# Random-feature attention and two feed-forward layers on one core: query tiles in slots among the keys and in half steps of the first group

## The chip, the core and the metric

The kernel runs on one core of a Trainium2 chip. The metric is the device time of one execution in microseconds. The engines are named as in the profile: PE is TensorE (PEld its weight loads), DVE is VectorE, ACT is ScalarE, POOL is GpSimd, and SP issues the DMAs.

## What is computed

The input has 4 batches of 576 rows, 8 heads of 64 columns. Cut to what matters:

```python
def phi(x):                                   # 128 random features of each head
    h = einsum('bhsd,md->bhsm', x, omega) - sum(x * x, -1, keepdims=True) / 2
    return exp(h - max(h, -1, keepdims=True)) / sqrt(m)
q_p, k_p = phi(q * scale), phi(k * scale)
kv = einsum('bhsm,bhsd->bhmd', k_p, v)        # needs every key of the batch
z = sum(k_p, axis=2)
x = einsum('bhsm,bhmd->bhsd', q_p, kv) / (einsum('bhsm,bhm->bhs', q_p, z)[..., None] + 1e-6)
# first layer, 512 -> 1536 -> 512, after a root-mean-square norm
g = xn @ w_gate
y = (g * sigmoid(g) * (xn @ w_val)) @ w_out
# second layer, 512 -> 2048 -> 512
h = y @ w_in
out = (h * cos(h)) @ w_out2
```

## The kernel before

The 2304 rows are 18 tiles of 128. A tile of keys ("k") is projected onto omega (`project`, L214: 16 matmuls into two PSUM banks), DVE takes the negated maximum of each head (L230), ACT the exponentials (L232), and `kv_product` (L388) adds the product with v into two banks of its batch. A tile of queries ("q") is projected the same way, its features are transposed (`transposed`, L239), copied out of PSUM (`keep_transposed`, L247 and L249), multiplied with kv (`sums`, L259), divided (`quotients`, L269 to L271), squared and normed (`square`, `root`, `norm`), transposed again (`turn`, L297) and put as two parts into a block `xhl` (`put`). Three tiles are a block of 384 rows; there are six blocks, and three buffers for them.

The weights come as float32 in integer form and are turned into a two-part form, chunk by chunk (68 chunks of 512 KB): one DMA, four DVE operations (L153 to L160), two of ACT (L138, L170), two of POOL. `Weights.tick` moves this work on by one of its seven turns a chunk; `pace` calls it at a rate. A finished chunk lies in a ring of RING buffers.

The feed-forward layers multiply two-part numbers with three matmuls a product (`mm3`, L446 to L448). The first layer goes over its 12 columns of 128 in three groups of four; in a group, for each of six blocks, each column is one step: 24 matmuls for gate and value (`gate_val`), then 12 for the output of the step before (`out1`), which accumulate in four banks. So a group has 24 steps. The second layer is 96 steps of 12 and 9 matmuls, in groups of 6, 5 and 5 columns.

The attention before runs in two parts. In the first, a loop over 27 tiles (18 of keys, 9 of queries, a k and a q in turn once the first nine keys are through) has its own PSUM pool (`banks_of(w=4, kv=2, q=2)`) and its own SBUF pool; each kv is also stored in DRAM (`kv_dram`, L435). Work of a tile is put off by whole passes of the loop with `after`. The loop ends only when its last query has gone through all its stages, and three blocks are then complete. Then the PSUM pool is closed and opened anew with `w=4, acc=4`; a second SBUF pool for queries is opened, kv and the norm's gain are loaded a second time (L473, L291), and nine queries run in steps 0 to 14 of the first group by the table `plan`, up to three stages of different tiles per step, after the two products of the step.

Every engine takes its instructions in the order in which the program writes them. SP issues all DMAs from one queue.

Of the kernel before, what the change touches and what calls it, by code (L numbers as in the profile page):

```python
# [33 lines left out]
F32 = mybir.dt.float32  # L34
# [4 lines left out]
AF = mybir.ActivationFunctionType  # L39
# [14 lines left out]
def attention_then_ffn(ctx: ExitStack, tc: tile.TileContext, qT, kT, v, omT, wc1, rms_g, wc2, out, B, H, S, D):  # L54
# [34 lines left out]
    banks = ExitStack()  # L89
    psum = [None, None]  # L90

    def banks_of(**tags):

        banks.close()
        psum[:] = banks.enter_context(tc.tile_pool(name="psum", bufs=1, space=PSUM, reuse_waits="tile")), tags

    def bank(tag, name):
        return psum[0].tile([P, 512], F32, tag=tag, name=name, bufs=psum[1][tag])
# [10 lines left out]
    kv_dram = [dram.tile([P, KVW], F32, name=f"kv_dram{b}") for b in range(B)]  # L109
# [89 lines left out]
    class Attention:  # L199
# [3 lines left out]

        def __init__(self, tile_of, tags, kv):
            self.tile_of, self.tags, self.kv, self.pool = tile_of, tags, kv, None
            self.raw, self.e, self.eT, self.x, self.ps, self.ms = {}, {}, {}, {}, {}, {}
            self.gain = None
# [6 lines left out]
        def project(self, nm, t):  # L214

            x = self.raw.pop((nm, t))
            ps = [bank(self.tags[0], f"{nm}p_ps{t}_{r}") for r in range(2)]
# [17 lines left out]
        def transposed(self, t, r):  # L235
            e = self.e.pop(("q", t, r))
            ps = bank(self.tags[1], f"eT_ps{t}_{r}")
# [4 lines left out]
        def keep_transposed(self, t, r):  # L242
# [3 lines left out]
            if self.pool is not None or r:  # L246
# [5 lines left out]
        def sums(self, t, r):  # L252

            eT = self.eT.pop((t, r))
            ps = bank(self.tags[1], f"num_ps{t}_{r}")
# [19 lines left out]
        def square(self, t):  # L275
            sq = self.tile_of("feat", [P, DM], F32, f"sq{t}")
# [12 lines left out]
        def load_gain(self):  # L289
            self.gain = self.tile_of("gain", [P, DM], F32, f"gain_{self.tags[1]}")  # L290
            nc.sync.dma_start(self.gain, rms_g.rearrange("(o c) -> o c", o=1).to_broadcast([P, DM]))  # L291

        def turn(self, t):
            a = self.x.pop(t)
            ps = self.ps["x", t] = bank(self.tags[0], f"xT_ps{t}")
# [27 lines left out]
    with tc.manual_schedule():  # L323

        banks_of(w=4, kv=2, q=2)
        with tc.tile_pool(name="att", bufs=2, side="right", reuse_waits="tile") as ap:
            depth = {"gain": 1, "raw": 4, "feat": 7, "featT": 4, "mx": 6, "den": 4}
            kv = [ap.tile([P, KVW], F32, name=f"kv{b}", bufs=1) for b in range(B)]
            NV = 3
            vt = [ap.tile([P, H + 1, D], F32, name=f"v{i}", bufs=1) for i in range(NV)]  # L330
            att = Attention(
                lambda what, shape, dt, name: ap.tile(shape, dt, tag=what, name=name, bufs=depth.get(what, 2)),
                ("w", "q"), kv)

            def load_v(t):
                if t < NTILE:
                    nc.sync.dma_start(vt[t % NV][:, 0:H], v[t])
# [7 lines left out]
            nc.sync.dma_start(om, omT)  # L345
            att.load(*tiles[0])
            att.load(*tiles[1])
            load_v(0)
            wts.tick(1)
            att.load(*tiles[2])  # L350
            load_v(1)
            load_v(2)
            att.load_gain()
            for a in vt:
                nc.vector.memset(a[:, H], 1.0)
            for a in kv:
                nc.vector.memset(a[:, H * (D + 1):], 0.0)
            make_identity(nc, ident)
            nc.gpsimd.memset(quarter, 0.25)
            nc.gpsimd.memset(half_pi, math.pi / 2)  # L360
            nc.gpsimd.memset(minus_half, -0.5)
            nc.vector.tensor_scalar(om, om, SCALE, None, op0=ALU.mult)

            acc, waiting, now = {}, {}, [0]

            def after(n, f, *args):

                waiting.setdefault(now[0] + n, []).append((f, args))

            def kv_products(t):  # L370

                e = [att.e.pop(("k", t, r)) for r in range(2)]
                for i, part in enumerate(parts(t)):
                    if i:
                        after(1, kv_product, t, e, *part)
                    else:
                        kv_product(t, e, *part)
                after(len(parts(t)), load_v, t + NV)

            def kv_product(t, e, b, p0, n):  # L380
                end = p0 + n + t * P == (b + 1) * S
                for r in range(2):
                    begin = (b, r) not in acc
                    if begin:
                        acc[b, r] = bank("kv", f"kv_ps{b}_{r}")
                    for h in range(HP):
                        hh = 2 * h + r
                        nc.tensor.matmul(  # L388
                            acc[b, r][:, h * P:(h + 1) * P], e[r][p0:p0 + n, h, :],
                            vt[t % NV][p0:p0 + n, hh::H - hh, :],  # L390
                            start=begin and h == 0, stop=end, skip_group_check=True)
                    if end:
                        keep_kv(b, r)

            def keep_kv(b, r):
                nc.vector.tensor_copy(
                    kv[b][:, 0:H * (D + 1)].rearrange("p (h two d) -> p two h d", two=2, d=D + 1)[:, r],
                    acc.pop((b, r)).rearrange("p (h c) -> p h c", c=P)[:, :, 0:D + 1])
                if r == 1:
                    after(1, nc.sync.dma_start, kv_dram[b], kv[b])  # L400

            UP = 15
            s = 0
            while s < len(tiles) or waiting:
                now[0] = s
                if s < len(tiles):
                    att.project(*tiles[s])
                    if s + AHEAD < len(tiles):
                        att.load(*tiles[s + AHEAD])
                if 0 <= s - 2 < len(tiles):  # L410
                    nm, t = tiles[s - 2]
                    if nm == "k":
                        kv_products(t)
                    else:
                        for r in range(2):
                            att.transposed(t, r)
                            after(0, att.keep_transposed, t, r)
                        for r in range(2):
                            after(1, att.sums, t, r)
                            after(1, att.quotients, t, r)  # L420
                        after(2, att.square, t)
# [354 lines left out]
```

## Time and profile before

| | |
|---|---|
| median of 3 runs | 1065.45 us (1064.0 to 1065.6) |
| profiled execution | 1066.04 us, span 1064.2 us |
| PE busy in the span | 95% |
| DVE, ACT, POOL busy | 59%, 44%, 18% |
| mean granted clock of TensorE | 0.987 |

Times below are in microseconds from the start of the span. PE's busy time is modelled from pipelined matmuls, so a stretch is judged by how long its known number of matmuls takes, and by what the idle time in it waited for.

### The profile page before, as it was taken

How to read it: one execution, taken by the hardware profiler on the slowest of the kernel's cores; microseconds unless marked ns; L12 is line 12 of the kernel's file. 1: busy time of each engine (PE TensorE's matmuls, PEld its weight loads, DVE VectorE, ACT ScalarE, POOL GpSimd, SP SyncE). 2: the span in 40 equal slices, each digit the busy share in tenths (PEclk: the TensorE clock that was granted, in tenths of full speed). 3: DMA queues.
4: the chain of work that ended last, by engine and by line, in shares of the span. 5: the costliest groups of instructions: out<-in, count | busy, mean ns of one | idle time of the engine just before them, and what ended most of it. 6: DMA issues, size and time to landing. Idle time of an engine off the chain costs nothing.

```text
span 1064.2 us, 15514 instructions
## 1 busy us (share of the span) xinstructions
PE 1015.5 (95%) x6040; PEld 956.5 (90%) x6040; DVE 632.6 (59%) x1185; ACT 464.9 (44%) x1005; POOL 195.2 (18%) x163
## 2 busy tenths in 40 slices
PE   6787869999999999999999999999999999999998
PEld 6776759999899999999999999999999888999997
DVE  6698743545452444432565644878766888656655
ACT  6576626466632222221233323555544444444443
POOL 3343101121111132220223210221101232000000
PEclk9899979999999999999999999999999999999999
DMA  7555241223132344440345342332220441103401
GB/s 259 210 182 168 110 171 60 71 74 115 50 110 109 135 152 149 149 158 1 103 175 222 115 159 89 129 119 99 99 79 22 173 163 61 60 1 110 156 32 59
DMA packets 33624, 123.96 MB, mean 116 GB/s; under 512 B 3728, under 2 KB 10000, under 8 KB 28944
## 3 DMA queue, kind: packets, MB, share of 16 engines
q1 hardware_dynamic: 33552, 122.99, 32.0%
q8 instruction: 47, 0.77, 0.3%
q14 instruction: 25, 0.20, 0.1%
HBM read 93.46 MB, written 29.51 MB: 116 GB/s over the span
## 4 chain that ended last, share of the span: by engine, by line
PE 77%; DVE 13%; ACT 5%; DMA 2%; issue 2%; SPq 0%; POOL 0%; ACTq 0%; DVEq 0%; POOLq 0%
PE gv_ps L447 9%; PE gv_ps L446 9%; PE gv_ps L448 9%; PE h_ps L448 5%; PE h_ps L446 5%; PE h_ps L447 5%; PE o_ps L447 5%; PE o_ps L448 5%; PE o_ps L446 5%; PE y_ps L446 5%; PE y_ps L447 4%; PE y_ps L448 4%; PE kv_ps L388 2%; PE num_ps L259 2%; DVE turns L592 1%
## 5 line engine op out<-in xcount | busy, mean ns | idle before, releaser
L446 PE MATMUL gv_ps<-xhl,w 128*128 128x384 f32 x576 | 194.1, 337 | 1.4 <-DVE xhl L309 1.4
L447 PE MATMUL gv_ps<-xhl,w 128*128 128x384 f32 x576 | 193.8, 336 | 0.0
L448 PE MATMUL gv_ps<-xhl,w 128*128 128x384 f32 x576 | 193.7, 336 | 0.0
L164 POOL TENSOR_TENSOR f<-f,raw 128x512 f32<-128x512 f32 x68 | 92.5, 1360 | 527.2 <-issue 325.7
L554 DVE TENSOR_TENSOR gv<-gv_ps,gv 128x384 f32<-128x384 f32 x72 | 40.1, 557 | 216.6 <-PE gv_ps L448 186.2
L448 PE MATMUL h_ps<-yhl,w 128*128 128x384 f32 x384 | 129.5, 337 | 0.0
L446 PE MATMUL h_ps<-yhl,w 128*128 128x384 f32 x384 | 129.2, 337 | 0.0
L447 PE MATMUL h_ps<-yhl,w 128*128 128x384 f32 x384 | 129.0, 336 | 0.0
L446 PE MATMUL o_ps<-w,o 128*128 128x512 f32 x288 | 112.4, 390 | 2.5 <-DVE osum L531 2.5
L448 PE MATMUL o_ps<-w,o 128*128 128x512 f32 x288 | 114.2, 397 | 0.2
L447 PE MATMUL o_ps<-w,o 128*128 128x512 f32 x288 | 113.7, 395 | 0.0
L172 POOL TENSOR_TENSOR w<-f,w 128x512 fp32r<-128x512 f32 x68 | 92.6, 1363 | 102.9 <-DVE t L557 49.0
L446 PEld LDWEIGHTS gv_ps<-xhl,w 128*128 128x128 f32 x576 | 109.3, 190 | 2.3 <-DVE xhl L309 1.8
L597 ACT ACTIVATE turns<-turns,half_pi 128x384 f32<-128x384 f32 x96 | 59.2, 617 | 115.6 <-DVE turns L592 115.6
L447 PEld LDWEIGHTS gv_ps<-xhl,w 128*128 128x128 f32 x576 | 109.1, 189 | 0.1
L448 PEld LDWEIGHTS gv_ps<-xhl,w 128*128 128x128 f32 x576 | 109.1, 189 | 0.0
L446 PE MATMUL y_ps<-t,w 128*128 128x384 f32 x288 | 98.9, 343 | 0.8 <-DVE y L519 0.8
L555 ACT CAST t<-gv 128x384 fp32r<-128x384 f32 x72 | 37.0, 514 | 143.4 <-DVE gv L554 143.4
L448 PE MATMUL y_ps<-t,w 128*128 128x384 f32 x288 | 96.8, 336 | 0.0
L447 PE MATMUL y_ps<-t,w 128*128 128x384 f32 x288 | 96.8, 336 | 0.0
L552 ACT ACTIVATE gv<-gv_ps 128x384 f32<-128x384 f32 x72 | 35.4, 492 | 140.4 <-PE gv_ps L448 136.5
L602 DVE TENSOR_TENSOR o<-turns,o 128x384 fp32r<-128x384 f32 x96 | 58.0, 604 | 47.6 <-ACT o L600 47.5
(75 smaller groups left out, 1797.1 us busy)
## 6 DMA issues: line engine op xcount, KB each, us to landing
raw<-wc SPq DMA_DIRECT2D x68, 512.0 KB, 3.6
yhl<-y_dram SPq DMA_DIRECT2D x14, 1536.0 KB, 6.9
xhl<-x_dram SPq DMA_DIRECT2D x10, 1536.0 KB, 7.1
x_dram<-xhl SPq DMA_DIRECT2D x6, 1536.0 KB, 6.1
y_dram<-yhl SPq DMA_DIRECT2D x6, 1536.0 KB, 5.4
kraw<-kT SPq DMA_DIRECT2D x18, 256.0 KB, 4.3
v<-v SPq DMA_DIRECT2D x18, 256.0 KB, 4.2
qraw<-qT SPq DMA_DIRECT2D x18, 256.0 KB, 4.1
```

Of the source, the lines that this page charges most:

```text
L164: nc.gpsimd.tensor_tensor(f32(f), f32(f), rest, op=ALU.add)
L172: nc.gpsimd.tensor_tensor(t[:, 1], self.f.pop(c - 1), f32(t[:, 0]), op=ALU.subtract)
L259: nc.tensor.matmul(ps[p0:p0 + n, h * P:(h + 1) * P], eT[:, h, p0:p0 + n], self.kv[b][:, at:at + P], start=True, stop=True, skip_group_chec ...
L388: nc.tensor.matmul(acc[b, r][:, h * P:(h + 1) * P], e[r][p0:p0 + n, h, :], vt[t % NV][p0:p0 + n, hh::H - hh, :], start=begin and h == 0, s ...
L446: nc.tensor.matmul(o, w[0], x[0], start=first, stop=False)
L447: nc.tensor.matmul(o, w[0], x[1], start=False, stop=False)
L448: nc.tensor.matmul(o, w[1], x[0], start=False, stop=last)
L552: nc.scalar.activation(a, ps[0], AF.Silu)
L554: nc.vector.tensor_tensor(a, ps[1], a, op=ALU.mult)
L555: nc.scalar.copy(t[:, 0], a)
L597: nc.scalar.activation(r, r, AF.Sin, bias=half_pi)
L602: nc.vector.tensor_tensor(o[:, 1], r, f32(o[:, 0]), op=ALU.subtract)
```

## The change

The attention's loop is replaced by slots. Slots 0 to 22 stand ahead of the first layer: 18 tiles of keys, and queries 0 to 4 in slots 6, 9, 12, 15 and 22. From there a slot is half a step of the first group (one product with its half of `out1`), and queries 5 to 17 begin in half steps 1, 3, 6, 9, 11, 14 and so on, 8/3 apart. Stage i of a query stands i slots after its projection, `kv_product` one slot after that of its keys. Stages 4 and 6 stand ahead of the slot's projection or product, all others behind it. Loads run two tiles ahead (three before), with three buffers (four before). Weights move on by four turns a slot until nine chunks are done (by five a pass until 15, before).

One PSUM pool of 4, 2 and 2 banks serves the whole kernel; the sums of the layers use the banks of "kv" and "q" in turn. From slot 23 on, all stages of a query use the four banks "w", which the products use too. One SBUF pool of the attention stays until the sums of the second group need its place, so kv and gain are loaded once. The ring has 22 buffers for 24. The second layer's groups have 5, 6 and 5 columns.

```diff
-    RING = 24
+    RING = 22
-    GROUPS2 = [range(0, 6), range(6, 11), range(11, 16)]
-    EARLY = 3 * TPB
+    GROUPS2 = [range(0, 5), range(5, 11), range(11, 16)]
...
+    BANKS = {"w": 4, "kv": 2, "q": 2}
+    psum = ctx.enter_context(tc.tile_pool(name="psum", bufs=1, space=PSUM, reuse_waits="tile"))
+    def bank_of_sums(name):
+        i = sums_taken[0]
+        sums_taken[0] += 1
+        return bank("kv" if i % 4 < 2 else "q", name)
...
-    kv_dram = [dram.tile([P, KVW], F32, name=f"kv_dram{b}") for b in range(B)]
...
-            depth = {"gain": 1, "raw": 4, "feat": 7, "featT": 4, "mx": 6, "den": 4}
+        depth = {"gain": 1, "raw": 3, "feat": 6, "mx": 6, "den": 4}
...
-            tiles = [("k", t) for t in range(TPP)]
-            for j in range(EARLY):
-                tiles += [("k", TPP + j), ("q", j)]
-            AHEAD = 3
+        tiles = {s: ("k", s) for s in range(6)}
+        tiles.update({6: ("q", 0), 9: ("q", 1), 12: ("q", 2), 15: ("q", 3), 22: ("q", 4)})
+        for t in range(6, NTILE):
+            tiles[next(s for s in range(99) if s not in tiles)] = ("k", t)
+        SLOTS = len(tiles)
+        for t in range(5, NTILE):
+            tiles[SLOTS + 1 + (8 * (t - 5)) // 3] = ("q", t)
+        for s, (nm, t) in tiles.items():
+            if nm == "k":
+                for i in range(len(parts(t))):
+                    then.setdefault(s + 1 + i, []).append((1, kv_product, t, i))
+            else:
+                for i in range(1, 7):
+                    then.setdefault(s + i, []).append((-i, query_step, t, i))
+        AHEAD = 2
+        def slot_before(s):
+            at = order.index(s) if s in tiles else -1
+            if at >= 0 and at + AHEAD < len(order):
+                att.load(*tiles[order[at + AHEAD]])
+            for k, f, *args in then.get(s, []):
+                if k in (-6, -4):
+                    f(*args)
+        def slot_after(s):
+            if s in tiles:
+                att.project(*tiles[s])
+                for r in range(2):
+                    att.features(*tiles[s], r)
+            for k, f, *args in then.get(s, []):
+                if k not in (-6, -4):
+                    f(*args)
         att.load(*tiles[0])
         att.load(*tiles[1])
         load_v(0)
         wts.tick(1)
-            att.load(*tiles[2])
         load_v(1)
         load_v(2)
         att.load_gain()
...
+        UP = 9
+        for s in range(SLOTS):
+            slot_before(s)
+            slot_after(s)
+            if wts.done < UP:
+                wts.tick(4)
+        att.tag = "w"
...
-            hid[n] = gate_val(blk, f, rate / 2)
-            for t, s in plan.get(n, []):
-                query_step(t, s)
+            if g == 0 and n < G:
+                rate = max(rate, 8)
+            s = SLOTS + 2 * n
+            slot_before(s)
+            ps = product(blk, f, 0)
+            a = silu(blk, f, ps)
+            slot_after(s)
             if n >= 1:
-                out1(g0, b0, f0, hid.pop(n - 1), st, en)
+                out1(*steps[n - 1][:3], hid[n - 1], *steps[n - 1][3:], (0, 1))
+            wts.pace(rate / 2)
+            flush(3)
+            slot_before(s + 1)
+            ps = product(blk, f, 1)
+            hid[n] = gated(blk, f, a, ps)
+            slot_after(s + 1)
+            if n >= 1:
+                out1(*steps[n - 1][:3], hid.pop(n - 1), *steps[n - 1][3:], (2, 3))
```

Three places in the instruction order show the move. In the names, `kp`/`qp` are projections, `kmx`/`qmx` maxima, `eT` transposed features, `num` the sums, `xT` the turned tile, `gv` and `y` the products and sums of the first layer; the first number is the tile or block.

SP, between the attention's first part and the first layer, before:

```order
L317 DMA x_dram0_1431<-xhl0_1052 128x3072
L435 DMA kv_dram3_77<-kv3_89 128x584
L317 DMA x_dram1_1629<-xhl1_1433 128x3072
L317 DMA x_dram2_1655<-xhl2_1631 128x3072
L291 DMA gain_w_1668<-rms_g 128x512
L473 DMA kv_in2_1670<-kv_dram2_76 128x584
L211 DMA qraw9_1672<-qT 128x512
L211 DMA qraw10_1731<-qT 128x512
L132 DMA raw19_1769<-wc1 128x1024
```

and of the change, around slots 20 to 23:

```order
L338 DMA v2_91<-v 128x512
L210 DMA qraw4_1121<-qT 128x512
L210 DMA qraw5_1162<-qT 128x512
L210 DMA qraw6_1197<-qT 128x512
L132 DMA raw13_1266<-wc1 128x1024
L210 DMA qraw7_1271<-qT 128x512
```

The first queries of the first group stood behind the stores of two blocks and reloads of the gain and of kv; they now follow the last keys directly.

DVE, in the attention's first part, before:

```order
L230 TENSOR_REDUCE qmx4_0_1036<-qp_ps4_0_1013 128x4
L153 TENSOR_SCALAR f13_1042<-W13_972 128x512
L155 SCALAR_TENSOR_TENSOR f13_1042<-W13_972,f13_1042 128x512
L230 TENSOR_REDUCE qmx4_1_1046<-qp_ps4_1_1014 128x4
L309 TENSOR_TENSOR xhl0_1052<-xT_ps0_981,xhl0_1052 128x4x128
L287 SCALAR_TENSOR_TENSOR x1_870<-x1_870,ms1_932,gain_q_109 128x512
L249 COPY eT3_0_1060<-eT_ps3_0_1025 128x512
L157 TENSOR_SCALAR raw13_822<-f13_1042 128x512
```

and of the change, in slots 15 and 16:

```order
L229 TENSOR_REDUCE qmx3_0_880<-qp_ps3_0_869 128x4
L229 TENSOR_REDUCE qmx3_1_887<-qp_ps3_1_870 128x4
L153 TENSOR_SCALAR f9_910<-W9_863 128x512
L155 SCALAR_TENSOR_TENSOR f9_910<-W9_863,f9_910 128x512
L281 TENSOR_SCALAR ms2_894<-ms2_894 128x1
L286 SCALAR_TENSOR_TENSOR x2_837<-x2_837,ms2_894,gain_106 128x512
L229 TENSOR_REDUCE kmx12_0_929<-kp_ps12_0_918 128x4
L229 TENSOR_REDUCE kmx12_1_936<-kp_ps12_1_919 128x4
L248 COPY eT3_0_947<-eT_ps3_0_942 128x512
```

The two maxima of a tile now stand together, the conversion behind them, and root and norm of the query before stand ahead of the next tile's maxima.

PE, in a step of the first group, before:

```order
L448 MATMUL gv_ps1_2_1_2178<-xhl1_1433,w7_689 128x384
L259 MATMUL num_ps11_0_2200<-kv_in2_1670,eT11_0_2140 128x128 x4
L259 MATMUL num_ps11_1_2205<-kv_in2_1670,eT11_1_2142 128x128 x4
L221 MATMUL qp_ps12_0_2222<-om_70,qraw12_2052 128x128
L221 MATMUL qp_ps12_1_2223<-om_70,qraw12_2052 128x128
```

and of the change, in a half step (the third of each eight):

```order
L220 MATMUL qp_ps12_1_2335<-om_73,qraw12_2037 128x128
L296 MATMUL xT_ps10_2358<-ident_72,x10_2171 128x128 x4
L258 MATMUL num_ps11_0_2364<-kv2_87,eT11_0_2292 128x128 x4
L258 MATMUL num_ps11_1_2374<-kv2_87,eT11_1_2299 128x128 x4
L461 MATMUL y_ps0_2_0_2_2303<-t2_0_2220,w2_421 128x384
```

The sums stood ahead of the next projection, behind two products; they now stand behind a projection and a turned tile, behind one product.

## Rows read from the trace of the kernel before

**Rows 1.** Busy time by stretch; columns: busy us (instructions) per engine, clock, DMA share, GB/s

```profile
0.00:12.00 12.00, 3.83 (x33) 3.59 (x33) 4.11 (x14) 4.73 (x11) 0.81 (x9) 1.00 0.82 274
0.00:149.70 149.70, 114.67 (x1020) 100.88 (x1020) 112.62 (x225) 93.28 (x286) 46.09 (x49) 0.95 0.51 178
50.00:130.00 80.00, 67.28 (x631) 58.18 (x631) 67.41 (x137) 54.02 (x171) 26.82 (x24) 1.00 0.44 153
130.00:149.70 19.70, 11.38 (x72) 9.34 (x70) 11.12 (x29) 8.42 (x22) 1.64 (x3) 0.81 0.23 95
149.70:161.20 11.50, 8.96 (x40) 8.59 (x40) 1.80 (x4) 1.69 (x3) 0.00 (x0) 0.65 0.70 231
161.20:352.70 191.50, 186.81 (x1228) 182.03 (x1225) 86.36 (x189) 98.66 (x209) 30.86 (x27) 0.99 0.24 82
...
352.70:652.20 299.50, 299.50 (x1730) 299.50 (x1729) 142.27 (x258) 83.60 (x166) 66.04 (x48) 1.00 0.38 140
652.20:1064.20 412.00, 405.59 (x2030) 365.51 (x2028) 289.50 (x511) 187.66 (x342) 52.25 (x39) 1.00 0.25 90
844.00:901.00 57.00, 54.29 (x266) 47.23 (x266) 47.26 (x82) 26.80 (x50) 17.50 (x13) 1.00 0.37 139
```

**Rows 2.** Timeline of SP, 126 to 166: start, duration, what it issued

```profile
139.05 11.11 SPq L317 DMA_DIRECT2D x_dram<-xhl  x2
...
151.67 2.20 SPq L211 DMA_DIRECT2D qraw<-qT  x2
```

**Rows 3.** Timeline of PE, 143 to 166; in brackets idle time before, and releaser

```profile
159.36 2.08 PE L221 MATMUL qp_ps<-om,qraw 64*128 64x128 f32 x16 [2.37 <-DMA qraw<-qT]
```

**Rows 4.** Chain of waits, in order of time: start, duration, what

```profile
4.01 7.81 DMA kraw<-kT
...
16.91 1.09 PE kp_ps L221 x16
18.00 1.98 PE kv_ps L388 x16
...
39.15 4.76 DMA v<-v
...
139.73 0.65 PE xT_ps L297 x4
...
207.57 1.78 PE num_ps L259 x16
209.36 1.09 PE qp_ps L221 x16
...
217.34 0.87 PE eT_ps L239 x8
```

**Rows 5.** Groups of instructions by line and shape: count, busy us, mean ns, idle before

```profile
L155 DVE SCALAR_TENSOR_TENSOR f<-W,f 128x512 int32<-128x512 int32 x68 | 51.1, 751 | 1.1
L160 DVE SCALAR_TENSOR_TENSOR raw<-raw 128x512 f32<-128x512 uint32 x68 | 46.9, 689 | 1.3
...
L554 DVE TENSOR_TENSOR gv<-gv_ps,gv 128x384 f32<-128x384 f32 x72 | 40.1, 557 | 216.6 <-PE gv_ps L448 186.2 <-ACT gv L552 24.1 <-issue 5.8
L153 DVE TENSOR_SCALAR f<-W 128x512 int32<-128x512 int32 x68 | 36.9, 543 | 5.7 <-ACT W L138 4.4 <-ACT w L170 1.1
...
L157 DVE TENSOR_SCALAR raw<-f 128x512 int32<-128x512 int32 x68 | 33.6, 495 | 1.2
...
L230 DVE TENSOR_REDUCE kmx<-kp_ps 128x4 f32<-128x512 f32 x36 | 23.9, 681 | 3.3 <-PE kp_ps L221 3.3
...
L531 DVE TENSOR_TENSOR osum<-o_ps,osum 128x512 f32<-128x512 f32 x36 | 23.2, 681 | 0.7 <-PE o_ps L448 0.7
```

**Rows 6.** Timeline of ACT in the first group: start, duration, what, idle time before

```profile
212.09 1.28 ACT L232 ACT_TABLE_LOAD   x1
213.39 2.17 ACT L232 ACTIVATE qe<-qp_ps,qmx 128x128 f32<-128x128 f32 x8
```

**Rows 7.** Busy time in one step of the first group; columns as in Rows 1

```profile
276.40:289.06 12.66, 10.79 (x62) 9.86 (x61) 5.80 (x13) 9.30 (x19) 1.81 (x2) 0.87 0.10 40
```

More of the change, by code (lines that the diff above doesn't have):

```diff
@@ L216, in project @@
             x = self.raw.pop((nm, t))
-            ps = [bank(self.tags[0], f"{nm}p_ps{t}_{r}") for r in range(2)]
+            ps = [bank("w", f"{nm}p_ps{t}_{r}") for r in range(2)]
             for i in range(HP):
@@ L323, in attention_then_ffn @@
     with tc.manual_schedule():
-        banks_of(w=4, kv=2, q=2)
-        with tc.tile_pool(name="att", bufs=2, side="right", reuse_waits="tile") as ap:
-            depth = {"gain": 1, "raw": 4, "feat": 7, "featT": 4, "mx": 6, "den": 4}
[L328 to L337, printed above, removed]
-            tiles = [("k", t) for t in range(TPP)]
-            for j in range(EARLY):
-                tiles += [("k", TPP + j), ("q", j)]
-            AHEAD = 3
[L345 to L349, printed above, removed]
-            att.load(*tiles[2])
[L351 to L381, printed above, removed]
-                for r in range(2):
[L383 to L421, printed above, removed]
-                        after(3, att.root, t)
-                        after(4, att.norm, t)
-                        after(5, att.turn, t)
-                        after(6, att.put, t, 0)
-                        after(6, att.put, t, 1)
-                        if t % TPB == TPB - 1:
-                            after(8, store, t // TPB, "x")
-                if s < len(tiles):
-                    att.features(*tiles[s], 0)
-                    if wts.done < UP:
-                        wts.tick(2)
-                    att.features(*tiles[s], 1)
-                for f, args in waiting.pop(s, []):
-                    f(*args)
-                if wts.done < UP:
-                    wts.tick(3)
-                s += 1
@@ new lines, in keep_kv, with query_step @@
+        def keep_kv(b, r):
+            nc.vector.tensor_copy(
+                kv[b][:, 0:H * (D + 1)].rearrange("p (h two d) -> p two h d", two=2, d=D + 1)[:, r],
+                acc.pop((b, r)).rearrange("p (h c) -> p h c", c=P)[:, :, 0:D + 1])
+        def query_step(t, s):
+            if s == 1:
+                for r in range(2):
+                    att.transposed(t, r)
+                    att.keep_transposed(t, r)
+            elif s == 2:
+                for r in range(2):
+                    att.sums(t, r)
+                    att.quotients(t, r)
+            elif s == 3:
+                att.square(t)
+            elif s == 4:
+                att.root(t)
+                att.norm(t)
+            elif s == 5:
+                att.turn(t)
+                att.put(t, 0)
+            elif s == 6:
+                att.put(t, 1)
+                if t % TPB == TPB - 1:
+                    store(t // TPB, "x")
@@ new lines, in attention_then_ffn @@
+        nc.sync.dma_start(om, omT)
+        att.load(*tiles[0])
+        att.load(*tiles[1])
+        load_v(0)
+        wts.tick(1)
+        load_v(1)
+        load_v(2)
+        att.load_gain()
+        for a in vt:
+            nc.vector.memset(a[:, H], 1.0)
+        for a in kv:
+            nc.vector.memset(a[:, H * (D + 1):], 0.0)
+        make_identity(nc, ident)
+        nc.gpsimd.memset(quarter, 0.25)
+        nc.gpsimd.memset(half_pi, math.pi / 2)
+        nc.gpsimd.memset(minus_half, -0.5)
@@ L569, in out1 @@
                 return
-            for e in range(KD):
+            for e in es:
                 if g == 0:
```

159 lines of the change are left out of this document (68 added, 91 removed).

## The prediction

> **What bounds the kernel now.** I read the busy time by stretch first, because the share of the whole span mixes stages with different limits. [rows 1] has four regimes. From 352.7 to 652.2 PE is busy for all 299.50 us: the second and third group of the first layer, 48 steps, so 6.24 us a step of 36 matmuls (2.08 a product, 1.04 half an output), and nothing but PE matters. The second layer, from 652.2 on, takes 412.0, and PE idles 6.4 of it; 2.7 of that lies between 844 and 901, where the conversion of weights runs beside three DVE additions a block. The first group takes 149.7 to 352.7, 203.0 us. The attention's first part takes 149.7 us, and there PE is not the limit: from 50 to 130 DVE is busy 67.41 of 80 us, 84%, and the last 19.7 us are a drain, with DVE at 56% and the clock at 0.81. Behind the drain stands a second hole: SP's queue is held 11.11 us by the stores of finished blocks [rows 2], the queries' loads are issued behind them at 151.67, and PE waits 2.37 us more for one at 159.36 [rows 3], with the clock at 0.65 over 149.7 to 161.2 [rows 1]. So the two places to look at are the first 161 us and the first group.
>
> **PE's cost of a query tile** is 0.87 transposes, 1.78 sums, 1.09 projection and 0.65 for the turned tile, 4.39 us [rows 4]. A key tile costs 1.09 + 1.98 = 3.07 [rows 4].
>
> **The first 23 slots.** Four pieces.
> - Start. The third tile of keys now lands at 4.01 + 7.81 = 11.8 [rows 4]. Three loads of 0.26 MB (two of v, the gain) are put ahead of it: 0.79 MB at 274 GB/s [rows 1] is 2.9 us, so 14.7. Slots 2 to 5 at PE's 3.07 end at 27.
> - Slots 6 to 17, four times q, k, k, limited by DVE. A conversion costs 0.543 + 0.751 + 0.495 + 0.689 = 2.48 a chunk [rows 5]. The part before has 112.6 us of DVE [rows 1]: less 36 key maxima of 0.681 (24.5) [rows 5], 16 conversions (39.6) and some 3 for kv's copies, nine queries leave 5.05 each. Three slots then have 4 x 0.681 + 5.05 + 12 turns of 7 (4.25) + 0.3 = 12.3 us. At DVE's share today, 84%, that is 14.6, four times 58.4: slot 18 begins at 85.
> - Slots 18 to 22 have no conversion: 5 x 3.07 plus 1.98 for the tile that two batches share is 17.4. **End at 102.8.**
> - Bounds: DVE at 95% of these slots gives 96; a wait for v as the one of 4.76 [rows 4] in each of two triples gives 113. I take 102.8, since the DVE share is measured in the same work.
> Removed without a price of their own: the stores of kv and their reloads, hidden but for their place in SP's queue.
>
> **The first group.** Now: 24 steps x 6.24 = 149.8, nine queries 39.5, sum 189.3 of 203.0, so 13.7 are lost. After: 149.8, thirteen queries 57.1, the transposes, sums and turn of query 4 (3.3): 210.2 without waits. What it loses I follow through one period of eight half steps with three tiles:
> - Transposes of the first tile wait for its exponentials. On DVE the product's multiply, ACT's cast and the subtraction (some 1.75 with the handover; 0.557 a pass of DVE [rows 5]) come first, then a maximum 0.68, then eight exponentials, 2.17 [rows 6]: 3.9 after the projection. PE has 1.04 of output and 2.08 of product to cover it, and half of the transposes: 0.3 lost.
> - In the third half step the four banks "w" are asked for by a product, two projections, a turned tile and two sums. The projection needs a bank that is free when ACT, done with the exponentials at 3.9, has squared a tile, reloaded the table (1.28 [rows 6]), done silu and copied, some 0.5 to 0.8 each: near 8, where PE is there at 7.3. I take 0.8.
> - There the second sums need a bank that DVE frees when it has divided the first. Its subtraction waits for a cast behind those copies, some 3 after the product, then two maxima 1.36 and the division 0.8: 5.2. PE is there after 0.8 + 1.09 + 0.65 + 0.89 = 3.4: 1.8 lost.
> - The other stages have over 4 us of cover: nothing.
> That is 2.9 a period; thirteen tiles are 4.33 periods, 12.6, and 1 for query 4 at the start: 13.6. Bounds: 0 (all covered), and for the top the step at 276.4: 12.66 us with 6.24 of the layer, 0.87 and 1.09 of a query, so 4.5 lost for a tile [rows 4, 7]; 13.75 tiles give 62. I take 13.6, near today's 13.7. **Group: 223.8.**
>
> Both together end at 326.6, against 352.7: **26 us less.**
>
> **The rest.** The output's halves stand 3.1 us (1.04 + 2.08) behind the product whose result they need, which is ready after some 2.0: nothing; without that cover up to 2 us a step. A ring of 22 puts two chunks of the second group into its first steps, three steps before they are read: 0, at worst 2. The second layer's first group converts 12 chunks in 30 steps where the second did 10 in 30: +5.0 us of DVE, less two additions of 0.681 for six blocks (8.2) [rows 5]; so the 2.7 us of waits move, 0 in sum, plus or minus 4.
>
> **Sum.** 1064.2 - 26.1 = 1038.1 span; the profiled execution took 1.8 more than its span, 1039.9, and was 0.6 above the median of the runs: **1039**.
>
> ACT's table is switched twice for each query, so 26 times in the first group where it was 18. [rows 6] shows a switch at 1.28 us, with the exponentials 1.30 after its start, and it stands mostly ahead of the maximum that is waited for anyway; so I cost the added switches at nothing but what the walk holds. The Trainium skill (ScalarE: Activation LUTs, What ACT_TABLE_LOAD costs, and the rule of its section on table sets to batch calls by set) speaks against mixing them: 1283 ns and a drain of some 1380 for every switch. By that each switch would hold ACT 1.38 longer, as an estimate up to 36 us over the group, 1075. The row has no such drain.
>
> **Rivals.**
> - *No waits in the first group* (0.17). For: PE ran 352.7 to 652.2 without one. Against: six banks asked of four. 1039 - 13 = 1026.
> - *Raw tiles late* (0.15). Two tiles ahead instead of three, in a queue that also waits for kv products and conversions. For: PE has waited 4.76 for v with more lookahead [rows 4]. Three such waits: 1053.
> - *DVE limits the second layer* (0.07). If all of the first 66 steps (283 us) lose as 844 to 901 does (2.71 of 57 [rows 1]), 13.5 instead of 2.7: 1050.
> - *Slower: the exponentials' chain stalls PE at each tile* (0.10). Place: the half step between projection and transposes, two switches of 1.28, eight exponentials, copies behind silu. Price: the step at 276.4 [rows 7], where switches, exponentials and transposes met, for every tile: 62 instead of 13.6, 1087. It decides from (13.6 + 26)/13.75 = 2.9 us lost a tile. The page named above would have it so, by its drain. Against: that step had the clock at 0.87 too, and other tiles of today lose about 1.
> That the order does not change as said can be left out: it is shown ahead.
>
> **Numbers.** Forecast 0.51, with its own range of 1030 to 1048. The range of 1025 to 1056 takes in it and the first three rivals, 0.90, less their tails. About 0.2% (2 us) can be told from no change. Faster 0.87, the same 0.03 (between the late-load and the slower case), slower 0.10.
>
> **What would show it.** In the changed profile the first product of the first layer stands near 103 us, with no drain ahead of it and no store of blocks ahead of its queries; DVE at 80 to 90% in slots 6 to 17; the second group begins near 327; the second and third group take 299.5 again; waits in the second layer move from its second to its first group. Wrong, if the first product is later than 115, or the first group longer than 240 us.

## The result, and the profile after

| | before | changed |
|---|---|---|
| median of the runs | 1065.53 us (1064.0 to 1065.81) | 1033.67 us (1033.41 to 1034.51) |
| span of the profiled execution | 1064.2 | 1032.7 |
| first product of the first layer begins | 149.7 | 102.72 |
| second group begins | 352.7 | 322.13 |
| second layer begins | 652.2 | 621.65 |

The ratio is 0.9705, with an interval of 0.9688 to 0.9722: 31.9 us less, where 26 were forecast. The time lies inside the stated range, and inside the narrower one given for the forecast (1030 to 1048).

These are the stretches that answer to [rows 1], cut where the changed kernel has its joints: the start, slots 6 to 17, slots 18 to 22, the first group, the second and third group, the second layer, and the 60 us of it in which PE waits. Busy time by stretch of the changed kernel, columns as in [rows 1]:

```profile
0.00:28.07 28.07, 21.09 (x175) 19.80 (x176) 14.86 (x33) 15.84 (x50) 6.29 (x14) 0.88 0.69 236
28.07:85.86 57.79, 48.02 (x449) 44.31 (x447) 45.65 (x95) 40.28 (x130) 20.82 (x18) 0.91 0.50 169
...
85.86:102.72 16.86, 16.86 (x182) 16.01 (x181) 9.93 (x18) 10.73 (x39) 0.55 (x1) 1.00 0.68 219
102.72:322.13 219.41, 210.54 (x1488) 203.05 (x1487) 117.57 (x259) 134.81 (x290) 41.10 (x40) 1.00 0.28 99
322.13:621.65 299.52, 299.52 (x1730) 299.52 (x1730) 148.79 (x258) 83.36 (x167) 64.17 (x48) 1.00 0.39 140
621.65:1032.70 411.05, 405.69 (x2029) 365.30 (x2028) 293.46 (x519) 189.75 (x347) 58.98 (x43) 1.00 0.26 93
640.00:700.00 60.00, 58.40 (x287) 50.80 (x286) 53.49 (x88) 32.82 (x63) 20.82 (x16) 1.00 0.40 141
```

Read it from the middle. In slots 18 to 22 PE is busy for all 16.86 us, at full clock, and the next matmul is already the first layer's: drain and hole of [rows 1, 2, 3] are gone. In the first group PE is idle for 8.87 of 219.41. Before that, in slots 6 to 17, no engine is full: PE 83%, DVE 79%, ACT 70%, and the clock is at 0.91. Of the 31.5 us of span, 30.6 are won by the time at which the second group begins; the second and third group take what they took (299.50 and 299.52), and the second layer 411.05 where it took 412.0.

What PE waits for in the first group (engine, line, what it waited for: us in total, times, longest):

```profile
PE num_ps L258 <- DVE x L270: 5.1, 3, 2.2
PE gv_ps L461 <- DVE den L268: 1.8, 2, 0.9
PE num_ps L258 <- DVE gv L526: 1.2, 1, 1.2
PE xT_ps L296 <- DVE gv L526: 0.4, 1, 0.4
PE num_ps L258 <- ACT eT L246: 0.4, 1, 0.4
```

And in slots 6 to 22:

```profile
PE xT_ps L296 <- ACT ke L231: 7.9, 3, 3.7
PE kp_ps L220 <- DMA kraw<-kT: 1.5, 1, 1.5
PE num_ps L258 <- ACT eT L246: 0.3, 1, 0.3
```

The largest is the turned tile, three times. The last one, in the order of DVE (timeline; start, duration, what, in brackets idle time before and releaser):

```profile
70.77 1.28 DVE L229 TENSOR_REDUCE qmx<-qp_ps 128x4 f32<-128x512 f32 x2
...
74.30 0.15 DVE L281 TENSOR_SCALAR ms<-ms 128x1 f32<-128x1 f32 x1 [1.20 <-ACT sq L277]
76.66 0.75 DVE L286 SCALAR_TENSOR_TENSOR x<-x,ms,gain 128x512 f32<-128x512 f32 x1 [2.21 <-POOL ms L282]
77.33 1.28 DVE L229 TENSOR_REDUCE kmx<-kp_ps 128x4 f32<-128x512 f32 x2
```

and of PE:

```profile
79.31 1.12 PE L296 MATMUL xT_ps<-ident,x 128*128 128x128 f32 x4 [3.65 <-ACT ke L231]
80.22 3.62 PE L258 MATMUL num_ps<-kv,eT 128*128 128x128 f32 x16
```

DVE stands 1.20 and 2.21 us for the square (behind the next query's eight exponentials on ACT) and for POOL's power, with two key maxima queued behind the norm. POOL does a subtraction of the conversion first:

```profile
74.85 1.27 POOL L172 TENSOR_TENSOR w<-f,w 128x512 fp32r<-128x512 f32 x1 [3.19 <-DMA v<-v]
76.08 0.55 POOL L282 TENSOR_TENSOR ms<-ms,minus_half 128x1 f32<-128x1 f32 x1
```

So 1.27 of the 2.21 is the conversion's. The keys' exponentials are late, their bank is late, and the turned tile, which wants it, holds PE for 3.65. The sums behind it take 3.62 where [rows 4] has 1.78, in a stretch (80.22 to 83.63) whose clock is 0.50.

### The profile page after: what moved, and what is told of

It is laid out like the page before. It is cut to its first block, busy times and chain, and to the rows that moved or that the text cites. A ratio compares the mean times of both kernels' runs of the same rounds, so it can differ in the third digit from the quotient of the medians.

```text
span 1032.7 us, 15416 instructions
## 1 busy us (share of the span) xinstructions
PE 1001.7 (97%) x6040; PEld 948.0 (92%) x6040; DVE 630.3 (61%) x1180; ACT 474.8 (46%) x1018; POOL 191.9 (19%) x163
## 3 DMA queue, kind: packets, MB, share of 16 engines
q1 hardware_dynamic: 32544, 120.93, 32.7%
## 4 chain that ended last, share of the span: by engine, by line
PE 72%; DVE 3%; ACT 1%; issue 0%; POOL 0%
PE gv_ps L462 8%; PE gv_ps L461 8%; PE gv_ps L463 8%; PE o_ps L463 6%; PE h_ps L463 6%; PE h_ps L461 6%; PE h_ps L462 6%; PE o_ps L462 6%; PE o_ps L461 6%; PE y_ps L461 4%; PE y_ps L462 4%; PE y_ps L463 4%; PE num_ps L258 1%; DVE o L574 1%; DVE turns L564 0%
## 5 line engine op out<-in xcount | busy, mean ns | idle before, releaser
L164 POOL TENSOR_TENSOR f<-f,raw 128x512 f32<-128x512 f32 x68 | 90.2, 1326 | 530.9 <-issue 304.2
L574 DVE TENSOR_TENSOR o<-turns,o 128x384 fp32r<-128x384 f32 x96 | 61.4, 639 | 47.0 <-ACT o L572 47.0
L572 ACT CAST o<-turns 128x384 fp32r<-128x384 f32 x96 | 49.3, 514 | 75.5 <-DVE turns L571 74.5
```

The lines of the kernel that those rows point to most:

```text
L164: nc.gpsimd.tensor_tensor(f32(f), f32(f), rest, op=ALU.add)
L572: nc.scalar.copy(o[:, 0], r)
L574: nc.vector.tensor_tensor(o[:, 1], r, f32(o[:, 0]), op=ALU.subtract)
```

## The experiments

Two questions: where the gain comes from, and what holds slots 6 to 17 and the first group, since neither looked quite as forecast. "First" is the start of the first layer's first product, "group" the length of its first group; both are from the traces. The ratio is to the kernel before, run beside each.

| run | median us | ratio (interval) | first | group |
|---|---|---|---|---|
| changed kernel | 1033.67 | 0.9705 (0.9688 to 0.9722) | 102.72 | 219.41 |
| nine early | 1038.44 | 0.9743 (0.9728 to 0.9759) | 130.61 | 195.23 |
| drain | 1042.55 | 0.9784 (0.9769 to 0.9800) | 111.59 | 218.88 |
| norm later | 1033.40 | 0.9696 (0.9677 to 0.9715) | 101.39 | 219.38 |
| norm later, everywhere | 1033.11 | 0.9695 (0.9680 to 0.9711) | 101.66 | 219.34 |
| fewer turns | 1032.83 | 0.9697 (0.9669 to 0.9724) | 101.55 | 219.43 |
| turned tile later | 1036.27 | 0.9712 (0.9685 to 0.9739) | 101.34 | 221.15 |
| norm later, fewer turns | 1032.00 | 0.9678 (0.9656 to 0.9701) | 98.67 | 220.91 |
| third load first | 1033.03 | 0.9696 (0.9665 to 0.9728) | 103.73 | 219.41 |
| exponentials last | 1045.10 | 0.9812 (0.9784 to 0.9841) | 102.39 | 229.39 |
| gaps 2, 2, 4 | 1035.89 | 0.9727 (0.9697 to 0.9757) | 104.02 | 220.12 |
| group's turned tile later | 1039.20 | 0.9739 (0.9712 to 0.9766) | 104.13 | 224.15 |
| groups 6, 5, 5 | 1037.99 | 0.9725 (0.9694 to 0.9756) | 104.02 | 219.40 |

Five of these kernels are the same up to their first product (the changed one, exponentials last, gaps, group's turned tile later, groups): it came at 102.39 to 104.13, 103.5 in the mean. So 1.7 us is what chance does in that stretch, and differences of "first" are read against it. Two places make it: the first tile of queries began at 26.96 to 29.32, and slots 6 to 11 took 25.1 in three of the five, at a clock of 1.00, but 26.5 in the two others (gaps, and group's turned tile later), at 0.94. Of the two with 26.5, the one with the gaps:

```profile
26.99:53.46 26.47, 24.24 (x232) 22.44 (x230) 21.27 (x46) 21.05 (x68) 9.62 (x8) 0.94 0.57 188
```

### Where the gain comes from: nine tiles early

```
-        tiles.update({6: ("q", 0), 9: ("q", 1), 12: ("q", 2), 15: ("q", 3), 22: ("q", 4)})
+        tiles.update({6 + 2 * j: ("q", j) for j in range(9)})
...
-        for t in range(5, NTILE):
-            tiles[SLOTS + 1 + (8 * (t - 5)) // 3] = ("q", t)
+        for t in range(9, NTILE):
+            tiles[SLOTS + 4 + (8 * (t - 9)) // 3] = ("q", t)
```

> Nine tiles of queries among the keys, every second slot from 6 to 22, instead of five, and nine instead of thirteen beside the first group. Theory J (the gain is the joint: no drain, no hole behind SP's stores): a tile early costs DVE 5.05 at 84% = 6.0 us, beside the first group it costs PE 4.39 and 0.7 of waits, so four tiles cost 24.0 - 20.4 = 3.6 more: 1037, with the first product near 127. Theory M (the gain is that tiles left the keys): most of the 31.5 comes back, 1055 to 1060.

1038.44, with the first product at 130.61 and a group of 195.23. Theory J holds: four tiles moved from the keys to the group are worth 27.9 earlier against 24.2 longer, 3.7 us in the traces (4.8 between the medians). This kernel has the nine early tiles of the kernel before and is still 27 us faster: 19 by its first product (130.6 to 149.7), 8 in the first group (195.2 to 203.0).

### And the drain by itself

```
-            tiles[SLOTS + 1 + (8 * (t - 5)) // 3] = ("q", t)
+            tiles[SLOTS + DRAIN + 1 + (8 * (t - 5)) // 3] = ("q", t)
...
-        for s in range(SLOTS):
+        for s in range(SLOTS + DRAIN):
...
-            s = SLOTS + 2 * n
+            s = SLOTS + DRAIN + 2 * n
```

with DRAIN = 6.

> The stages of the fifth tile of queries run to their end, in six slots without other work, before the first product; all else as in the changed kernel. Theory J: the chain of that one tile costs some 14 us (maxima and exponentials 3.5, transposes and copies 2, sums and quotients 3.4, square, root and norm 3, turned tile 2), of which 3.3 of PE leave the first group: about 10.5 more, 1044. Theory M: the drain is cheap, since PE's work in it is only moved: 1034 to 1037.

1042.55, 8.9 us more than the changed kernel, as Theory J had it (10.5). Busy time from the fifth tile's projection to the first product, in this kernel:

```profile
100.95:111.59 10.64, 7.20 (x77) 6.27 (x77) 5.19 (x13) 5.14 (x18) 0.55 (x1) 0.92 0.03 10
```

No engine is above 68%, and DVE and ACT are half empty, as in the drain of [rows 1]: one tile's chain, from engine to engine, with little beside it. A part of the price falls behind the drain, in the first group of this kernel:

```profile
111.59:330.47 218.88, 212.15 (x1442) 204.00 (x1441) 115.20 (x250) 131.90 (x281) 40.59 (x39) 0.98 0.28 99
```

PE is busy 212.15 there, where the changed kernel, with 3.3 us more to do, is busy 210.54; the clock is 0.98 instead of 1.00. So of the 30.6 us, some 9 are the drain and 4 the moved tiles. Some 18 are left. By the run with nine early, they lie by 8 in the first group and by 10 ahead of it (19 less the drain). The first group with nine tiles beside it, in the kernel before and in that run:

```profile
149.70:352.70 203.00, 195.78 (x1264) 190.62 (x1265) 88.17 (x193) 100.34 (x212) 30.86 (x27) 0.97 0.27 90
130.61:325.84 195.23, 191.81 (x1287) 185.89 (x1286) 100.42 (x211) 107.12 (x229) 38.37 (x35) 1.00 0.28 98
```

PE is idle 3.4 us instead of 7.2, and busy 4.0 less at the higher clock. The hole behind SP's stores stood in this stretch (11.5 us long, PE idle 2.5 of it, at a clock of 0.65), but no run puts the stores back alone. The 10 ahead of the first product stay open, and one rival there is not tested: six conversions fewer are done among the keys. At the prediction's 2.48 they are 14.9 us of DVE, and by its share of 84% 17.7 us of time, more than what is left. No run kept them there, so how much of the 10 is the new order and how much the moved conversions is not shown.

### What holds slots 6 to 17: the norm behind the maxima

```
-                if k in (-6, -4):
+                if k == -6 or (k == -4 and s >= SLOTS):
```

(and the reverse in `slot_after`).

> Same instructions; among the keys the root and the norm of a query stand behind the two maxima of the slot's tile on DVE instead of ahead of them. Theory A (the order on DVE holds the slots): the two triples of slots that took 16.2 and 16.6 us take some 12.5 as the first one did, so the first product of the first layer comes some 7.8 us earlier, near 95, and the time is 1026. Theory B (DVE's amount of work holds the slots, as the prediction had it): DVE does the same work, the first product stays within 1 us of 102.7 and the time within 1 us of 1033.7.

The first product came at 101.39, 2.1 before the mean of the five; the time did not move by an amount that can be told. Theory A's 7.8 fell, and so did B's nothing. The waits of PE in its slots 6 to 22:

```profile
PE xT_ps L296 <- DVE x L286: 4.9, 3, 1.9
PE kp_ps L220 <- DMA kraw<-kT: 2.0, 1, 2.0
```

Against the rows of the changed kernel the turned tile no longer waits for a bank; it waits for the norm, 4.9 instead of 7.9.

The same order beside the first group as well (`if k == -6:` alone):

> The same order also beside the first group: root and norm behind the half step's maxima, casts and products. Theory A: as the run before, and the 1.6 us in which PE waits in the first group for the gate's multiply (1.2 and 0.4) go too: 1024.5. Rival: the norm is late for the turned tile, whose blocks are read on time only just, and each of four blocks costs 0.5 to 1: 1028 to 1030.

1033.11; the 1.2 for the gate's multiply is gone from the list, 0.5 more for the division stands in its place, and the group is 219.34: nothing.

### Fewer turns of the conversion

```
-                wts.tick(4)
+                wts.tick(3 if 6 <= s < 18 else 4)
```

> In slots 6 to 17 three turns of the conversion a slot instead of four, in the slots behind them four until nine chunks are done (before: none there). Theory B (DVE's amount of work holds slots 6 to 17): 3 of 12 turns of a triple leave, 1.06 us of DVE, at 84% 1.26, four times 5.0; the slots behind are held by PE and take the turns for nothing: first product near 97.7, time 1029. Theory A (waits between engines hold them, not the amount): 0 to -1.

The first product came at 101.55, 1.9 before the mean, not 5: between the theories. Slots 12 to 17 became 28.8 us where they were 32.7 (32.7 to 33.8 in the five). Busy time by stretch, first of the changed kernel:

```profile
53.14:85.86 32.72, 25.11 (x218) 23.39 (x217) 24.60 (x50) 20.63 (x65) 11.22 (x10) 0.84 0.44 145
```

then of this run:

```profile
53.74:82.56 28.82, 23.92 (x217) 22.09 (x217) 21.63 (x45) 18.36 (x61) 6.60 (x7) 0.88 0.43 147
```

3.0 us of DVE left them, and 3.9 of time, of which 1.2 is PE's busy time, at a clock of 0.88 instead of 0.84. But slots 6 to 11 took 27.0, at a clock of 0.94, where two of the five took 26.5 at that clock; and slots 18 to 22, which now convert, went from 16.9 to 19.0: those were not free.

### The turned tile a slot later

```
-                    then.setdefault(s + i, []).append((-i, query_step, t, i))
+                    then.setdefault(s + i + (i > 4 and t < 4), []).append((-i, query_step, t, i))
```

with the norm behind the maxima.

> As the run with the norm behind the maxima, and the turned tile and its two copies of the first four tiles of queries one slot later. Theory C (what holds slots 6 to 17 is neither DVE's amount nor its order alone, but that PE stands at the turned tile, first for a bank, 7.9 us, then with the norm moved for the norm, 4.9): both waits go, the slots from the first to the fifth tile of queries take 69.1 - 4.9 = 64 us, the first product comes near 97, the time is 1028. Rival (the engines' work and the lower clock fill the slots, and a wait removed here comes back at the next stage): 69 us again, 1032 to 1033.

From the first to the fifth tile 71.65 us: the rival. PE's waits in its slots 6 to 22:

```profile
PE num_ps L258 <- DVE eT L248: 7.0, 3, 2.4
PE kp_ps L220 <- DVE kmx L229: 1.4, 1, 1.4
```

Both waits for the turned tile are gone, and 7.0 stand before the sums instead, for a copy that is now late in DVE's queue. Theory C fell: the wait moves to whatever comes next.

### Norm later and fewer turns together

Both edits above.

> Norm behind the maxima and three turns of the conversion a slot together (each was made alone). Theory D (in slots 12 to 17 two limits lie side by side: the chain from a tile of queries' projection through its square, root and norm to the next maxima, and DVE's queue; with one gone the other holds): together they give more than the 1.2 and 0.8 us by which the first product came earlier alone, the two triples take about 13 each, the first product stands at 95 to 97, the time is 1027 to 1028. Rival (what is left is neither: loads of keys behind the weights' loads in SP's queue, and the lower clock behind each wait): the first product stays at 100 or later, the time at 1031 or above.

98.67: 4.8 before the mean of the five, where the two alone gave 2.1 and 1.9, and between the bounds that had been set. In slots 12 to 17 the two add up: 30.5 (norm), 28.8 (turns), 26.5 (both) against 32.7, that is 2.2 and 3.9, and 6.2 together. This run's slots 12 to 17:

```profile
54.51:81.05 26.54, 22.78 (x217) 20.92 (x217) 22.65 (x45) 18.67 (x61) 6.14 (x6) 0.94 0.49 160
```

PE's busy time fell from 25.11 to 22.78 with the clock at 0.94 instead of 0.84, so some 2.3 of the 6.2 came by the clock; whether the edits raised it is not shown. By these sums it was not that one limit hid behind the other; in these slots work and waits of DVE stand in one chain, and each piece taken out shortens it. The rival has a small part. Slots 6 to 11 took 27.1 where the changed kernel took 25.1; but the clock there was 0.94, at which two of the five took 26.5, so some 0.6 is left for this row of PE (the changed kernel waits 1.84 for the turned tile in these slots):

```profile
47.66 1.56 PE L220 MATMUL kp_ps<-om,kraw 64*128 64x128 f32 x16 [2.60 <-DMA kraw<-kT]
```

and these of SP's queue, in the same run:

```profile
39.90 0.33 SPq L338 DMA_DIRECT2D v<-v  x1
41.58 0.33 SPq L132 DMA_DIRECT2D raw<-wc  x1
41.96 0.42 SPq L210 DMA_DIRECT2D kraw<-kT  x1
```

The keys are issued right behind a load of weights, which stood in the queue for 1.3 us until the slower conversion gave back a buffer. Of the 4.8, 1.5 is lost again in the first group, which takes 220.91 at a clock of 0.99 with the same waits as the changed kernel's. The median is 1032.0 (1030.45 to 1033.96), the lowest of all; its interval overlaps the changed kernel's, so by the runs it is not shown to be faster.

### The start

```
+        att.load(*tiles[2])
         load_v(1)
         load_v(2)
```

(with the same load left out of slot 0).

> The third tile of keys is loaded ahead of the second and third tile of v and the gain. Theory of the prediction (the three loads put ahead of it cost 2.9 us at the start): the third projection begins near 10.7 instead of 13.5, everything behind it 2.9 earlier, 1031. Rival: the tile of v that is now later is waited for instead, 1033.7.

1033.03, and a first product at 103.73: nothing, as the rival said. The load of the third tile of keys was issued at 4.01 instead of 5.47, but its projection did not come near 10.7; it began at 12.79, against 13.04 to 14.68 in the five kernels named above:

```profile
12.79 1.16 PE L220 MATMUL kp_ps<-om,kraw 64*128 64x128 f32 x16 [3.12 <-DMA kraw<-kT]
```

The first tile of queries began at 26.91; in runs with the loads as changed it began anywhere from 26.70 to 29.41.

### The first group: exponentials behind the sums

In `slot_after`, for s >= SLOTS, the call of `features` stands behind the loop over the stages instead of ahead of it.

> Beside the first group the projected tile's maxima and exponentials stand behind the slot's other stages, so the division of another tile's first sums stands ahead of the two maxima on DVE. Theory A (the prediction's third loss: the second sums wait for a bank that DVE frees behind two maxima): each of the three waits of PE for the division (5.1 in all, 2.2 the longest) is shorter by some 1.3, the first group 215.5 instead of 219.4, the time 1030. Rival: the exponentials, now behind the sums, come some 2 later, and the transposes of the next half step wait for them: the first group 219 to 222, 1033 to 1036.

1045.10, 11 us more by the medians, and a group 10 us longer. Waits in its first group, the largest of PE's matmuls and the largest of its weight loads:

```profile
PE num_ps L258 <- DVE x L270: 3.1, 3, 1.0
...
PEld eT_ps L238 <- ACT qe L231: 6.8, 9, 1.7
```

The maxima ahead of the division were indeed a part of that wait: it falls from 5.1 to 3.1. But the transposes, for which neither matmul nor weight load waits in the changed kernel's group, now wait nine times for exponentials. The rival was right in kind and too small. (The list of the matmuls alone has 2.2 for these: where an engine loads ahead, its loads have to be asked too.)

### The first group: fewer banks asked for at once

```
-            tiles[SLOTS + 1 + (8 * (t - 5)) // 3] = ("q", t)
+            tiles[SLOTS + 1 + 8 * ((t - 5) // 3) + (0, 2, 4)[(t - 5) % 3]] = ("q", t)
```

> The tiles of queries beside the first group begin 2, 2 and 4 half steps apart instead of 2 or 3 and 3, so a turned tile never meets a projection and sums in one half step, but a projection meets sums in two half steps of eight instead of one. Theory A (what costs is the division behind the maxima of a projected tile, wherever the two meet): two waits of 1.5 to 2.2 a period instead of one, some 5 to 7 more, 1039 to 1041. Theory B (what costs is that six banks are asked of four): five at most, so the waits go, 1029.

```
-            tiles[SLOTS + 1 + (8 * (t - 5)) // 3] = ("q", t)
+            tiles[SLOTS + (8 * (t - 5)) // 3] = ("q", t)
...
-                    then.setdefault(s + i, []).append((-i, query_step, t, i))
+                    then.setdefault(s + i + (i > 4 and t > 4), []).append((-i, query_step, t, i))
```

> Beside the first group the turned tile and its copies of tiles 5 to 17 come one half step later, and these tiles begin one half step earlier; so no half step asks the four banks for more than five. Theory B (the waits for the division, 5.1, come from six banks asked of four): they go, the first group takes 214 to 215, the time 1029. Rival, as with the gaps of 2, 2 and 4: other waits for a bank (for silu, for the division) take their place, 219 to 220, 1033 to 1034.

Groups of 220.12 and 224.15. With gaps of 2, 2 and 4 PE waits in the first group for:

```profile
PE gv_ps L461 <- ACT gv L521: 3.0, 4, 1.1
PE gv_ps L461 <- DVE den L268: 2.8, 3, 1.0
```

with the turned tile later for:

```profile
PE gv_ps L461 <- ACT gv L521: 4.0, 4, 1.8
PE gv_ps L461 <- ACT qe L231: 2.3, 1, 2.3
PE num_ps L258 <- ACT gv L521: 1.4, 3, 0.5
```

In both the 5.1 for the division is gone, although in the first a projection meets sums twice as often. So it takes six banks asked of four in one half step to make that wait, as Theory B had it; the maxima ahead of the division, moved in the run before, lengthen it. But neither gained: products now stand for banks that silu, the exponentials or the division frees.

### The second layer's groups

```
-    GROUPS2 = [range(0, 5), range(5, 11), range(11, 16)]
+    GROUPS2 = [range(0, 6), range(6, 11), range(11, 16)]
```

> The groups of the second layer as before (6, 5 and 5 columns of blocks instead of 5, 6 and 5), all else as changed. Theory (PE's waits in the second layer only move between its first and second group, 0 in sum): the second layer takes 411 to 412.5, PE waits 1.5 to 3 in it, now in the second group; the time within 1.5 of 1033.7. Rival (the new groups are worth the 1 us by which the second layer became shorter, or more, since a chunk fewer stands in the ring): 1035 to 1037.

The rival, and more. In this run's trace, 3.7 us longer than the changed kernel's, 1.3 are the later first product and 2.4 the second layer, which took 413.46, where it took 411.1 in every other run with the new groups. There PE waits for:

```profile
PE o_ps L461 <- DVE osum L502: 1.8, 1, 1.8
PE h_ps L461 <- ACT w L170: 0.7, 1, 0.7
PE h_ps L463 <- POOL w L172: 0.7, 1, 0.7
```

The changed kernel waits 0.6, 0.5 and 0.4 there, 1.5 in all against 3.2. So beside a ring of 22 the new groups are worth 2.4 us, of which these lists show 1.7; the other 0.7 is PE's busy time, at a clock of 0.99 instead of 1.00. The two waits of 0.7 are, 20 us into the layer, for weights whose conversion is not done. The kernel before, with the old groups and a ring of 24, took 411.9.

## Why the prediction was right, point by point

- **The first 23 slots**: forecast to end at 102.8, ended at 102.72, and each piece came within 1.1: start 28.07 (27), slots 6 to 17 57.79 (58.4), slots 18 to 22 16.86 (17.4). That the sum is met to 0.1 is luck: five runs of this stretch spread over 1.7, and errors cancel inside it. (Its bound of 113 adds up to 112.3.) For the last piece the reason was right as well: PE is full. For the middle one the sum was right for half a reason. "Slots 6 to 17, limited by DVE at 84%" gave the length, but no triple of slots took the 14.6: the first two triples took 12.5 each, the last two 16.4.

```profile
28.07:53.14 25.07, 22.91 (x233) 20.92 (x231) 21.05 (x46) 19.66 (x66) 9.61 (x8) 1.00 0.58 201
```

  In the first two DVE has its 84%, but 10.5 us of work a triple where the sum has 12.3; in the last two (53.14 to 85.86, shown above) it has the 12.3 and a share of 75%. Over all it is busy 79%, just under the 80 to 90 that were to show it. A quarter of the conversion's turns taken out gave 1.9 us where that step has 5.0, and an edit that leaves DVE's amount as it was gave the same. DVE is full of work and of waits inside its own order, and a share taken from like work contains both. So it foretells the length of work put together in the same way, not what an edit gains.
- **The start's 2.9** for three loads put ahead: not seen when the order was put back. The third tile began at 13.54, not 14.7; what brought the start to 28.07 all the same is, for the most part, that its projection and product took 5.73 where the sum has 3.07, at half the clock:

```profile
13.54:19.27 5.73, 5.72 (x33) 5.28 (x33) 3.44 (x6) 3.78 (x13) 1.87 (x2) 0.50 0.46 149
```

- **The first group**: forecast 223.8, measured 219.41. The base of 210.2 held: PE is busy 210.54. Of the losses, 13.6 by the walk, 8.9 came. "There the second sums need a bank that DVE frees when it has divided the first" was the right place and the right size, 1.7 in the mean where the walk had 1.8:

```profile
163.98 1.13 PE L258 MATMUL num_ps<-kv,eT 128*128 128x128 f32 x8 [2.16 <-DVE x L270]
203.75 1.13 PE L258 MATMUL num_ps<-kv,eT 128*128 128x128 f32 x8 [1.30 <-DVE x L270]
245.30 1.13 PE L258 MATMUL num_ps<-kv,eT 128*128 128x128 f32 x8 [1.62 <-DVE x L270]
```

  But it was counted for 4.33 periods, and a projection, a turned tile and sums meet in three half steps only, in the second to the fourth period: 5.1 instead of 7.8. The other two terms, "0.3 lost" at the transposes and the projection's bank ("I take 0.8"), came to nothing in the list of matmuls: 4.8 less. The start of the group, put at 1, lost 3.0 in three waits by 124.82 (0.89, 1.20 and 0.95), and two waits of 0.4 stand in no term. So 7.5 too much in the period's terms and 2.8 too little in the rest make the 4.7 by which the walk was too long.
- **Table switches at nothing but the walk.** Right: on ACT, beside the first group,

```profile
242.64 1.28 ACT L231 ACT_TABLE_LOAD   x1
243.93 2.18 ACT L231 ACTIVATE qe<-qp_ps,qmx 128x128 f32<-128x128 f32 x8
```

  the exponentials begin 1.29 behind the load's start, and no wait of PE in the group is for exponentials. The Trainium skill (ScalarE: Activation LUTs, What ACT_TABLE_LOAD costs) has a drain of some 1380 ns for every switch to a different set; these rows leave no room for one, and the measurement decides.
- **The rest, 0 plus or minus 4**: the second and third group 299.52, the second layer 0.95 shorter. The waits moved from its second to its first group as said: the 60 us from 640 on hold 1.60 of PE's idle time, and DVE is busy 53.49 there. "0 in sum" is two sizes that nearly cancel: with 22 buffers and the old groups the layer takes 1.6 more than before (413.46 and 411.9), a price of the ring that the prediction does not have there, and the new groups win back 2.4. No run has the new groups beside a ring of 24.
- **The rivals**: *no waits in the first group* (1026) fell, 8.9 stayed. *Raw tiles late* (1053) came once behind the start, 1.5 us. *DVE limits the second layer* did not come. *Slower by the exponentials' chain* (2.9 us lost a tile) fell at 8.9 for 13 tiles, 0.7 a tile.

The forecast's span was 5.4 us too long: 4.4 in the first group, by the terms above, and 0.95 in the second layer. So the mechanism held where the runs test it, in the drain and in the first group's wait for a bank; how well the first 23 slots and the second layer add up was in part luck.

## What to carry to other kernels

When stages that hand work to each other are cut by a drain, price the drain by one item's whole chain through all engines (here 9 us): running the first items of the next stage into it gives that back, whatever becomes of the engine shares. Where no engine is full (83% at most in slots 6 to 17) and PE waits in turn for a bank, a norm or a copy, a wait removed can come back at the next instruction in order; here the amount of work and the order eased together gave in their slots what each gave alone, added up. Count the banks that a half step asks for against those there are, but move stages only with the whole period in view: three reorderings here (turned tile later, gaps, group's turned tile later) each removed the wait they aimed at, and none gained. And when two kernels differ by a microsecond or two, compare the granted clock of the stretch before a cause is named.

## What the runs showed of the hardware that was not expected

DVE and POOL get in each other's way. The norm of one tile took 0.75 us at 76.66, shown above, and of another, on DVE:

```profile
59.86 1.77 DVE L286 SCALAR_TENSOR_TENSOR x<-x,ms,gain 128x512 f32<-128x512 f32 x1 [0.67 <-POOL ms L282]
```

where POOL had begun an addition 0.07 us earlier:

```profile
59.79 1.29 POOL L164 TENSOR_TENSOR f<-f,raw 128x512 f32<-128x512 f32 x1
```

It ends 0.55 behind POOL's end, and takes 1.0 us longer than the other. The Trainium skill (SBUF — State Buffer, SBUF: two separate sides) says that the two engines share a pair of ports as an exclusive lock, and that whichever starts first holds it for its whole instruction, where VectorE's has two inputs in SBUF, as this one has, and GpSimd's reads SBUF. These rows agree, but for some 0.2 us, since 0.55 is less than the 0.75 that the norm takes alone. A mean duration from a table of groups contains such stands: the prediction's 0.543 for the conversion's first pass is a mean of passes, and single ones here take 0.42 where POOL is idle.
